# Split pieces stored by SP, early mixed tokens in a shared 8 KB buffer, and weights' high words in PSUM, in an attention and mixer kernel on one Trainium2 core

## The chip, the cores and the metric

The kernel runs on one core of one Trainium2 chip. The core has five engines that run side by side, each with its own list of instructions in fixed order: PE (matrix products, results into PSUM), DVE and ACT (elementwise work on SBUF and PSUM), POOL (elementwise work on SBUF) and SP (here it only issues DMA transfers). An engine waits at an instruction until the data or the buffer that it needs is there, and all that stands behind it on that engine waits too. The metric is the device time of one execution in microseconds (us); less is better.

## The reference, cut to what matters

Three blocks follow each other; all is fp32, B = 4, S = 576.

```python
# attention: 4 x 8 heads of 64, S = 576
scores = scale * q @ k.T + minimum(-(cum[:, None] - cum[None, :]), 0)   # causal
attn = softmax(scores)
x = (attn @ v)                                       # -> [4, 576, 512]
# mixer 1 (d_model 512, d_ff 1024)
xk = mu_k * x + (1 - mu_k) * x_prev                  # x_prev: x one token earlier
xr = mu_r * x + (1 - mu_r) * x_prev
k = maximum(xk @ w_k, 0)
x = sigmoid(xr @ w_r) * (k * k @ w_v)
# mixer 2
u = x + (maximum(x.T @ w_tok1, 0) @ w_tok2).T
out = u + maximum(u @ w_ch1, 0) @ w_ch2
```

## The kernel before, in words

Products of fp32 accuracy are made of three products of split numbers: a value is stored as a high part in the format fp32r and a low part (the rest), and `products` adds high x high, high x low and low x high. The weights come from the host as float64, read as pairs of 32-bit words. `weight_load` brings a piece (128 partitions x 512 values for w_k and w_r, x 256 for w_v) to SBUF, and `weight_split` makes high and low parts of it: ACT scales the high words (`high`) and the low words in place, DVE joins them with two shift-and-or instructions (lines 572 and 573), ACT copies the sum to the high part, and the rest is subtracted (line 577, POOL for w_k and w_r, DVE for w_v; w_v is halved first, by a copy of ACT).

Order of the work: the first batch's 8 heads are done twice over. `early` makes the first 256 queries of each head from plain fp32 products; `late` makes queries 256 to 575. Then 24 `visits` (the heads of batches 1 to 3, in pairs) do all 576 queries with split products (`scores`, `transposes`, `values`). Among them stand the products of mixer 1 (`up` gives the tile `h`, `gate` gives `r`, `down` gives `vd`), and later mixer 2. The order in each engine's list is set by a scheduler from places given by hand (`with at(...)`); it is fixed before the run.

The places that the change touches:

- `keep_busy` adds products whose result nobody reads (tile `idle`, in a PSUM bank of the pool `ps_d`), 4 after each of the 16 transposes of `early` and 3 after those of the first three heads of `late`.
- `mix` makes a tile of mixed tokens (`XK` for k, `XR` for r) with four operations: lines 478 and 479 on DVE, the high part on ACT (480), the low part on DVE (481). For the first chunk (256 tokens of batch 0) its four tiles are placed at N0 = 16, behind the early heads. `up` needs all four.
- `load` and `split` prepare the queries and keys of a pair of visits in four pieces of 128x288: SP loads a piece (`qkr`, two buffers), ACT copies the high part, POOL subtracts (line 224, `qkp`, two buffers) and POOL issues the store to DRAM (`hl_d`, line 225). `place` loads them back as the tiles `X` (lines 251 to 254, on SP), and `scores` uses these.
- The queries and keys of the first four early heads (`HL`) lie in 8 KB per partition of the pool `cp`.

Of the kernel before, what the change touches and what calls it, by code (L numbers as in the profile page):

```python
# [24 lines left out]
def attention_moe_mixer(  # L25
# [59 lines left out]
    ps_d = ctx.enter_context(tc.tile_pool(name="ps_d", bufs=2, space=PSUM, reuse_waits="tile"))  # L85

# [11 lines left out]
    act = {"ps": ps_d}  # L98
# [45 lines left out]
    xt = {}  # L144
# [7 lines left out]

    def keep_busy(n, x, w):
        for _ in range(n):
            nc.tensor.matmul(act["idle"][:, 0:w], x[:, 0:128], x[:, 0:w], start=True, stop=True)  # L155
# [8 lines left out]
    def bias_rows(cp):  # L164
# [3 lines left out]
        cum = cp.tile([G, S], F32, name="cum")  # L168
# [38 lines left out]

    def part(y):
        x, c = divmod(y, 2)
        return x, S * c // 2, S * (c + 1) // 2  # L210

    def load(i, y):
        g = visits[i][0]
        x, c0, c1 = part(y)
        t = qk_raw[i, y] = qk_p.tile([128, S // 2], F32, tag="raw", name="qkr", bufs=2)
        nc.sync.dma_start(out=t, in_=qk[g:g + 2, :, x, c0:c1].rearrange("h d s -> (h d) s"))

    def split(i, y):
# [3 lines left out]
        e = qk_p.tile([128, 2, S // 2], F32, tag="parts", name="qkp", bufs=2)  # L222
        copy("A", e[:, 1].bitcast(F32R), t)
        nc.gpsimd.tensor_tensor(out=e[:, 0], in0=t, in1=e[:, 1], op=ALU.subtract)
        nc.gpsimd.dma_start(out=hl_d[g:g + 2, :, 2 * x:2 * x + 2, c0:c1].rearrange("h d t s -> (h d) t s"), in_=e)
# [85 lines left out]
    def early(h, j, V0, cp):  # L311
# [14 lines left out]
        keep_busy(4, P, 128)  # L326
# [31 lines left out]
    def late(h, j):  # L358
# [19 lines left out]
        if h < 3 and m == 128:  # L378
            keep_busy(3, P, 128)
# [91 lines left out]

    def mix(b, c, i, p):
        dst = act[("XK", "XR")[i]]
# [3 lines left out]
        t = act["sm"].tile([128, CM], F32, tag="t", name="t", bufs=3)  # L477
# [5 lines left out]
    def up(b, c, m):  # L483
        n = width(c)
        kk, x = act["KK"], act["XK"]
# [81 lines left out]
    def weight_split(key, hi, lo, half=0):  # L567
        t = raw.pop(key)
        low, high = t[:, :, :, 0], t[:, :, :, 1]
        copy("A", f32(high), f32(high), 2.0 ** -112)  # L570
        nc.scalar.activation(out=low.bitcast(U32), in_=low.bitcast(U32), func=AF.Copy, scale=TOP3, bias=-0.496)  # L571
        nc.vector.scalar_tensor_tensor(out=low, in0=high, scalar=3, in1=low, op0=ALU.logical_shift_left, op1=ALU.bitwise_or)  # L572
        nc.vector.scalar_tensor_tensor(out=low, in0=high, scalar=-2 ** 31, in1=low, op0=ALU.bitwise_and, op1=ALU.bitwise_or)  # L573
        if half:
            copy("A", f32(low), f32(low), 0.5)
        copy("A", hi, f32(low))
        (nc.vector if half else nc.gpsimd).tensor_tensor(out=lo, in0=f32(low), in1=f32(hi), op=ALU.subtract)
# [91 lines left out]
    act["idle"] = ps_d.tile([128, 512], F32, tag="d", name="idle")  # L669
# [4 lines left out]
    early_at.append((cp.tile([128, 8 * QC], F32, name="HL"), 0, 4))  # L674
# [299 lines left out]
```

## Time and profile before

| | us |
|---|---|
| median of 3 runs | 893.46 (891.07 to 894.57) |
| the profiled execution, its own time | 887.59 |
| its span, first to last instruction | 885.8 |
| PE busy | 847.3 (96%) |
| DVE busy | 535.2 (60%) |
| ACT busy | 469.8 (53%) |
| POOL busy | 347.9 (39%) |

A busy time is the sum over an engine's instructions in the span. The shares are means over stages with different limits, so they are read by stretches of time below. The granted clock is the mean TensorE clock that the chip gave, as a share of 2.4 GHz.

### The profile page before, as it was taken

To read this page: it belongs to the slowest core of one execution; us is meant where nothing else is said; L and a number is where in the kernel's file an instruction comes from. 1 tells how busy PE (TensorE), PEld (TensorE's weight loads), DVE (VectorE), ACT (ScalarE), POOL (GpSimd) and SP (SyncE) were. 2 spreads that over 40 slices of the span, in tenths; PEclk is the share of its full clock that TensorE was granted. 3 is DMA by queue.
4 is the path that set the end of the run, shared out by engine and by line. 5 is a ranking of instruction groups with operands and counts; after the bars stand their busy time and mean duration, and the time that the engine had idled before them with its cause. 6 is when DMAs were issued, how large, how long until landed. Compare 5 with 4: busy or idle time off the path is not lost.

```text
span 885.8 us, 17817 instructions
## 1 busy us (share of the span) xinstructions
PE 847.3 (96%) x6185; PEld 793.4 (90%) x6185; DVE 535.2 (60%) x1583; ACT 469.8 (53%) x1320; POOL 347.9 (39%) x510
## 2 busy tenths in 40 slices
PE   7969999999789999999989899999999999999998
PEld 5736677998679999999989899899999999999998
DVE  4896897677899677996657866871331322222321
ACT  3877976866776765868456775760320211211210
POOL 3676876877773433645244674650000000000000
PEclk8969999999999999999999999999999999999999
DMA  7975667578753334441132656653022112112100
GB/s 195 255 207 170 205 188 215 163 215 245 199 159 85 82 79 107 100 121 48 50 100 80 206 157 197 208 186 124 25 71 63 44 40 66 38 42 67 43 25 24
DMA packets 78730, 108.37 MB, mean 122 GB/s; under 512 B 11072, under 2 KB 59200, under 8 KB 78640
## 3 DMA queue, kind: packets, MB, share of 16 engines
q1 hardware_dynamic: 68352, 77.40, 32.0%
q0 software_dynamic: 8416, 29.24, 10.2%
q8 instruction: 49, 0.80, 0.4%
q10 hardware_dynamic: 1872, 0.59, 0.4%
q14 instruction: 41, 0.34, 0.1%
HBM read 77.74 MB, written 28.90 MB: 120 GB/s over the span
## 4 chain that ended last, share of the span: by engine, by line
PE 70%; DVE 9%; DMA 7%; ACT 5%; issue 4%; POOL 3%; SPq 0%; ACTq 0%; POOLq 0%; DVEq 0%
PE c L110 32%; PE vd L110 8%; PE h L110 7%; PE r L110 4%; PE t L110 3%; PE t L411 3%; PE pv L463 3%; DMA hl_d<-qkp 2%; DMA raw<-in_moe_w_ch_dram 2%; DVE raw L572 2%; PE s L286 2%; PE pv L397 2%; PE s L287 2%; DVE raw L573 1%; PE s L368 1%
## 5 line engine op out<-in xcount | busy, mean ns | idle before, releaser
L813 ACT ACTIVATE HID<-c 128x256 fp32r<-128x256 f32 (+1 forms) x96 | 39.4, 410 | 218.7 <-PE c L110 218.5
L274 POOL TENSOR_SCALAR P<-P,sum 64x576 f32<-64x576 f32 (+4 forms) x160 | 101.2, 636 | 94.1 <-DVE sum L273 41.9
L110 PE MATMUL h<-XK,WK 128*128 128x256 f32 (+1 forms) x768 | 124.5, 302 | 4.1 <-ACT k L490 2.0
L110 PE MATMUL vd<-KK,WV 128*128 128x256 f32 (+1 forms) x768 | 121.6, 300 | 0.0
L110 PEld LDWEIGHTS h<-XK,WK 128*128 128x128 f32 x768 | 106.6, 188 | 10.1 <-ACT k L490 3.1
L271 ACT ACTIVATE P<-P,mx 64x576 f32<-64x576 f32 (+4 forms) x160 | 95.9, 600 | 28.5 <-DVE mx L261 27.5
L110 PEld LDWEIGHTS vd<-KK,WV 128*128 128x128 f32 x768 | 106.8, 188 | 1.7 <-issue 0.7
L110 PE MATMUL c<-U,WK 128*128 128x256 f32 (+1 forms) x768 | 102.6, 291 | 2.1 <-DVE HID L814 2.1
L110 PE MATMUL c<-HID,WV 128*128 128x256 f32 (+1 forms) x768 | 104.4, 291 | 0.0
L110 PEld LDWEIGHTS c<-U,WK 128*128 128x128 f32 x768 | 98.7, 188 | 2.4 <-DVE HID L814 2.3
L110 PEld LDWEIGHTS c<-HID,WV 128*128 128x128 f32 x768 | 100.4, 188 | 0.0
L814 DVE SCALAR_TENSOR_TENSOR HID<-c,HID 128x256 fp32r<-128x256 f32 (+1 forms) x96 | 43.9, 457 | 83.3 <-ACT HID L813 83.2
L878 DVE TENSOR_TENSOR ut<-c,ut 128x256 f32<-128x256 f32 (+1 forms) x32 | 14.7, 458 | 119.9 <-PE c L110 112.5
L261 DVE CUSTOM_DVE_ANT_0 P<-s,maskc 64x288 f32<-64x288 f32 (+4 forms) x160 | 74.9, 474 | 16.9 <-PE idle L155 4.4
L493 POOL TENSOR_TENSOR KK<-k,KK 128x256 fp32r<-128x256 f32 (+1 forms) x64 | 53.5, 837 | 34.7 <-ACT k L492 29.2
L110 PE MATMUL r<-XR,WR 128*128 128x320 f32 (+1 forms) x384 | 61.4, 302 | 2.6 <-ACT k L490 2.6
L75 ACT ACTIVATE raw<-raw 128x256 f32<-128x256 f32 (+2 forms) x101 | 46.8, 466 | 29.4 <-DMA raw<-in_moe_w_ch_dram 9.7
L572 DVE SCALAR_TENSOR_TENSOR raw<-raw 128x256 int32<-128x256 int32 (+2 forms) x85 | 49.7, 584 | 19.8 <-ACT raw L571 16.6
L110 PEld LDWEIGHTS r<-XR,WR 128*128 128x128 f32 x384 | 53.9, 192 | 3.6 <-ACT k L490 2.9
L411 PE MATMUL t<-ident,P 128*128 128x128 f32 (+1 forms) x360 | 52.8, 262 | 3.5 <-DVE PT L440 2.4
L110 PE MATMUL c<-HID,WR 128*128 128x256 f32 (+1 forms) x384 | 54.5, 291 | 0.0
L573 DVE SCALAR_TENSOR_TENSOR raw<-raw 128x256 int32<-128x256 int32 (+2 forms) x85 | 52.9, 624 | 1.2
(116 smaller groups left out, 1695.9 us busy)
## 6 DMA issues: line engine op xcount, KB each, us to landing
X<-hl_d SPq DMA_DIRECT2D x72, 288.0 KB
hl_d<-qkp POOLq DMA_DIRECT2D x48, 288.0 KB, 4.2
raw<-in_moe_w_ch_dram POOLq DMA_DIRECT2D x48, 256.0 KB, 3.7
qkr<-in_qk_dram SPq DMA_DIRECT2D x48, 144.0 KB
yt<-y_d SPq DMA_DIRECT2D x16, 288.0 KB
u_d<-yt SPq DMA_DIRECT2D x16, 288.0 KB
raw<-in_moe_w_k_dram SPq DMA_DIRECT2D x8, 512.0 KB
raw<-in_moe_w_v_dram SPq DMA_DIRECT2D x16, 256.0 KB
```

The costliest lines, as they stand in the source:

```text
L75: nc.scalar.activation(out=out, in_=in_, func=AF.Copy, scale=scale)
L110: nc.tensor.matmul(ps, a, b, start=first and i == 0, stop=last and i == n - 1)
L261: nc.vector.tensor_tensor_reduce(out=P[0:m, c0:c1], in0=ps[0:m, 0:c1 - c0], in1=maskc[0:m, 512 - q0 + c0:512 - q0 + c1], scale=-scale, sca ...
L271: nc.scalar.activation(out=P[0:m, 0:w], in_=P[0:m, 0:w], func=AF.Exp, bias=mx[0:m, x:x + 1], scale=-1.0, accum_out=sm[0:m, 0:1])
L274: nc.gpsimd.tensor_scalar(out=P[0:m, 0:w], in0=P[0:m, 0:w], scalar1=sm[0:m, 1:2], scalar2=1.0, op0=ALU.mult, op1=ALU.mult)
L411: nc.tensor.transpose(ps[0:r, p0 + m * k:p0 + m * k + m], P[0:m, 128 * k:128 * k + r], ident[0:m, 0:m])
L463: nc.tensor.matmul(ps[:, o:n], vv[:, k, :], part, start=(k == 0 and t == 0), stop=(k == nk - 1 and t == len(parts) - 1),)
L493: nc.gpsimd.tensor_tensor(out=kk[:, 1, m, 0:n], in0=t[:, 0:n], in1=f32(kk[:, 0, m, 0:n]), op=ALU.subtract)
L572: nc.vector.scalar_tensor_tensor(out=low, in0=high, scalar=3, in1=low, op0=ALU.logical_shift_left, op1=ALU.bitwise_or)
L573: nc.vector.scalar_tensor_tensor(out=low, in0=high, scalar=-2 ** 31, in1=low, op0=ALU.bitwise_and, op1=ALU.bitwise_or)
L813: nc.scalar.activation(out=hi, in_=ps, func=AF.Relu)
L814: nc.vector.scalar_tensor_tensor(out=lo, in0=ps, scalar=0.0, in1=f32(hi), op0=ALU.max, op1=ALU.subtract)
```

## The change

- The two banks of `ps_d` are no longer open from the start. In the first stage a pool `ps_w` has them, and for w_k and w_r ACT writes the scaled high words there (`high`) and not in place; the two DVE instructions read `high` from PSUM. `ps_d` opens after it. The `idle` tiles come from `ps_t`, the pool of the transposes; there are 3 and not 4 per early transpose, and only the first late head has any.
- One buffer of 8 KB (tag `HX`) is used in turn for the queries and keys of the first four early heads (`HE`), for the mixed k tokens of the first chunk (`HX`) and for all raw and split pieces of the visits (`PB`). Each user waits until the one before has been read.
- The first chunk's mixed tokens are placed among the early heads (3.5, 5.5, 7.5 and so on) and not behind them.
- Halving w_v goes into the copy to the high part (its scale) and into the subtraction, which becomes a multiply and subtract on DVE. One ACT copy per piece goes.
- The store of a split piece is issued by SP and not by POOL.

```diff
     def keep_busy(n, x, w):
+        idle = ps_t.tile([128, 512], F32, tag="t", name="idle")
         for _ in range(n):
-            nc.tensor.matmul(act["idle"][:, 0:w], x[:, 0:128], x[:, 0:w], start=True, stop=True)
+            nc.tensor.matmul(idle[:, 0:w], x[:, 0:128], x[:, 0:w], start=True, stop=True)
...
+    def stage():
+        if "PB" not in act:
+            act["PB"] = qk_p.tile([128, 8 * QC], F32, tag="HX", name="PB")
+        return act["PB"]
...
-        t = qk_raw[i, y] = qk_p.tile([128, S // 2], F32, tag="raw", name="qkr", bufs=2)
+        t = qk_raw[i, y] = stage()[:, y % 2 * S // 2:(y % 2 + 1) * S // 2]
         nc.sync.dma_start(out=t, in_=qk[g:g + 2, :, x, c0:c1].rearrange("h d s -> (h d) s"))
...
-        e = qk_p.tile([128, 2, S // 2], F32, tag="parts", name="qkp", bufs=2)
+        e = stage()[:, S + y % 2 * S:S + y % 2 * S + S].rearrange("p (t s) -> p t s", t=2)
         copy("A", e[:, 1].bitcast(F32R), t)
         nc.gpsimd.tensor_tensor(out=e[:, 0], in0=t, in1=e[:, 1], op=ALU.subtract)
-        nc.gpsimd.dma_start(out=hl_d[g:g + 2, :, 2 * x:2 * x + 2, c0:c1].rearrange("h d t s -> (h d) t s"), in_=e)
+        nc.sync.dma_start(out=hl_d[g:g + 2, :, 2 * x:2 * x + 2, c0:c1].rearrange("h d t s -> (h d) t s"), in_=e)
...
-        keep_busy(4, P, 128)
+        keep_busy(3, P, 128)
...
-        if h < 3 and m == 128:
+        if h < 1 and m == 128:
             keep_busy(3, P, 128)
...
+    def mixed(b, c, i):
+        if (b, c, i) == (0, 0, 0):
+            if "HX" not in act:
+                act["HX"] = qk_p.tile([128, 2 * KD * QC], F32R, tag="HX", name="HX")
+            return act["HX"].rearrange("p (t k s) -> p t k s", t=2, k=KD)
+        return act[("XK", "XR")[i]]
+
     def mix(b, c, i, p):
-        dst = act[("XK", "XR")[i]]
+        dst = mixed(b, c, i)
...
-    def weight_split(key, hi, lo, half=0):
+    def weight_split(key, hi, lo, half=0, ps=None):
         t = raw.pop(key)
         low, high = t[:, :, :, 0], t[:, :, :, 1]
-        copy("A", f32(high), f32(high), 2.0 ** -112)
+        if ps is None:
+            copy("A", f32(high), f32(high), 2.0 ** -112)
+        else:
+            bank = ps.tile([128, high.shape[1], high.shape[2]], I32, tag="w", name="high")
+            copy("A", f32(bank), f32(high), 2.0 ** -112)
+            high = bank
         nc.scalar.activation(out=low.bitcast(U32), in_=low.bitcast(U32), func=AF.Copy, scale=TOP3, bias=-0.496)
         nc.vector.scalar_tensor_tensor(out=low, in0=high, scalar=3, in1=low, op0=ALU.logical_shift_left, op1=ALU.bitwise_or)
         nc.vector.scalar_tensor_tensor(out=low, in0=high, scalar=-2 ** 31, in1=low, op0=ALU.bitwise_and, op1=ALU.bitwise_or)
+        copy("A", hi, f32(low), 0.5 if half else 1.0)
         if half:
-            copy("A", f32(low), f32(low), 0.5)
-        copy("A", hi, f32(low))
-        (nc.vector if half else nc.gpsimd).tensor_tensor(out=lo, in0=f32(low), in1=f32(hi), op=ALU.subtract)
+            nc.vector.scalar_tensor_tensor(out=lo, in0=f32(low), scalar=0.5, in1=f32(hi), op0=ALU.mult, op1=ALU.subtract)
+        else:
+            nc.gpsimd.tensor_tensor(out=lo, in0=f32(low), in1=f32(hi), op=ALU.subtract)
...
-    early_at.append((cp.tile([128, 8 * QC], F32, name="HL"), 0, 4))
+    early_at.append((qk_p.tile([128, 8 * QC], F32, tag="HX", name="HE"), 0, 4))
...
+        if h % 2 == 1 and h > 1:
+            with at(2 * h + 1.5):
+                for p in range(2) if h == 3 else (h // 2,):
+                    mix(0, 0, 0, p)
...
-            weight_split((nm, f), W[:, 0, :, f:f + 128], W[:, 1, :, f:f + 128])
+            weight_split((nm, f), W[:, 0, :, f:f + 128], W[:, 1, :, f:f + 128], ps=ps_w)
...
-    with at(N0):
-        for p in range(KD):
-            mix(0, 0, 0, p)
```

In the changed file the lines shift: 155 (fillers) is 157, 110 (products) is 108, 261 (row maximum) is 268, 368 and 377 (late scores and transposes) are 375 and 384, 478 to 481 (mix) are 492 to 495, 571 to 573 (shift and or) are 592 to 594, 577 is 597 and 599.

How the order changes, at three places. First PE, where the products `h` of the first chunk begin (`s<-X` and `t<-ident,P` are scores and transposes of `late`, `pv` its values). Before:

```order
L377 MATMUL t<-ident,P_923 128x128 x3
L155 MATMUL idle<-P_923 128x128 x3
L377 MATMUL t<-ident,P_965 128x128 x4
L155 MATMUL idle<-P_965 128x128 x3
L377 MATMUL t<-ident,P_984 128x64 x4
L377 MATMUL t<-ident,P_984 64x64
L368 MATMUL s<-X_510 64x288
L110 MATMUL h<-XK,WK 128x256 x4
L368 MATMUL s<-X_513 128x384
L110 MATMUL h<-XK,WK 128x256 x3
```

and after the change:

```order
L404 MATMUL pv<-PT_801,VV_536 64x64
L384 MATMUL t<-ident,P_925 128x128 x3
L108 MATMUL h<-HX,WK 128x256 x18
L384 MATMUL t<-ident,P_964 128x128
L108 MATMUL h<-HX,WK 128x256
```

`h` moves ahead of the second late head's last transposes and score, as one block of 18, and the fillers of that head are gone.

Second DVE, among the early heads, at a weight piece of w_k (`raw` is its buffer). Before:

```order
L77 COPY xt<-pv 128x256
L273 RECIPROCAL sum<-sum 128x1
L572 SCALAR_TENSOR_TENSOR raw<-raw 128x512
L261 ISA P_319,mx<-s,maskc 128x128
L261 ISA mx 128x1
L272 TENSOR_SCALAR sum<-sum 128x1
L573 SCALAR_TENSOR_TENSOR raw<-raw 128x512
```

and after the change:

```order
L492 TENSOR_SCALAR t<-xt,mu 128x256
L279 TENSOR_SCALAR sum<-sum 128x1
L493 SCALAR_TENSOR_TENSOR t<-xt,omu,t 128x256
L280 RECIPROCAL sum<-sum 128x1
L279 TENSOR_SCALAR sum<-sum 128x1
L268 ISA P_332,mx<-s,maskc 128x128
L268 ISA mx 128x1
L280 RECIPROCAL sum<-sum 128x1
L593 SCALAR_TENSOR_TENSOR raw<-high,raw 128x512
L268 ISA P_348,mx<-s,maskc 128x256
L268 ISA mx 128x1
L495 TENSOR_TENSOR HX<-t,HX 128x256
```

The operations of a mixed token tile stand here now, and the shift-and-or reads `high`. Third the pieces: before, POOL's list, among the last early heads and the first late one:

```order
L224 TENSOR_TENSOR qkp<-qkr,qkp 128x288 x2
L225 DMA hl_d<-qkp 128x2x288
L274 TENSOR_SCALAR P_448<-P_448,sum 128x256
L225 DMA hl_d<-qkp 128x2x288
L274 TENSOR_SCALAR P_791<-P_791,sum 128x384
```

and after the change SP's list, at the sixth late head, where the first pieces are loaded:

```order
L258 DMA X_1448<-ext_d 4x1152
L223 DMA PB<-in_qk_dram 128x288 x2
L575 DMA raw<-in_moe_w_v_dram 128x2x256 x2
L360 DMA VV_1244<-in_v_dram 128x4x128
L361 DMA VV_1244<-in_v_dram 64x128
L232 DMA hl_d<-PB 128x2x288
L223 DMA PB<-in_qk_dram 128x288
L232 DMA hl_d<-PB 128x2x288
L223 DMA PB<-in_qk_dram 128x288
```

The stores stand between the loads of SP, and the first piece comes at the sixth late head and not before the first.

## Rows read from the trace of the kernel before

**Rows 1.** The page, part 1: busy us, share of the span, instructions.

```profile
PE 847.3 (96%) x6185; PEld 793.4 (90%) x6185; DVE 535.2 (60%) x1583; ACT 469.8 (53%) x1320; POOL 347.9 (39%) x510
```

**Rows 2.** Busy us of PE, PEld, DVE, ACT, POOL by stretch; clock; DMA share, GB/s.

```profile
20.00:47.40 27.40, 27.25 (x177) 20.73 (x176) 22.64 (x73) 23.88 (x60) 18.99 (x24) 1.00 0.98 263
47.40:71.40 24.00, 15.75 (x74) 8.90 (x72) 20.58 (x42) 17.24 (x44) 18.12 (x18) 0.72 0.62 181
71.40:136.40 65.00, 63.33 (x391) 45.70 (x392) 55.06 (x152) 52.20 (x156) 45.52 (x62) 1.00 0.66 196
200.00:260.00 60.00, 52.97 (x372) 47.13 (x371) 50.72 (x197) 47.33 (x141) 46.37 (x68) 0.97 0.79 214
```

**Rows 3.** Waits of PE, 47.4 to 71.4 us: total us, times, longest.

```profile
PE s L368 <- DVE mx L261: 7.2, 3, 3.1
```

**Rows 4.** Timeline of DVE: start us, duration us, instruction.

```profile
40.48 0.68 DVE L261 CUSTOM_DVE_ANT_0 P<-s,maskc 128x512 f32<-128x512 f32 x1
...
47.21 2.60 DVE L572 SCALAR_TENSOR_TENSOR raw<-raw 128x512 int32<-128x512 int32 x1 [0.60 <-ACT raw L571]
...
56.65 0.68 DVE L572 SCALAR_TENSOR_TENSOR raw<-raw 128x512 int32<-128x512 int32 x1
...
64.07 0.96 DVE L573 SCALAR_TENSOR_TENSOR raw<-raw 128x512 int32<-128x512 int32 x1
```

**Rows 5.** Groups by form, 0 to 160 us: count, busy us, mean ns, idle before.

```profile
L75 ACT ACTIVATE raw<-raw 128x256 f32<-128x256 f32 x32 | 13.9, 439 | 11.0 <-DMA raw<-in_moe_w_v_dram 8.6 <-DVE raw L573 2.2
L577 DVE TENSOR_TENSOR WV<-raw,WV 128x256 fp32r<-128x256 f32 x16 | 12.8, 801 | 1.3 <-ACT WV L75 1.3
L572 DVE SCALAR_TENSOR_TENSOR raw<-raw 128x512 int32<-128x512 int32 x12 | 12.4, 1037 | 1.0 <-ACT raw L571 1.0
L573 DVE SCALAR_TENSOR_TENSOR raw<-raw 128x512 int32<-128x512 int32 x12 | 11.6, 971 | 0.1
...
L261 DVE CUSTOM_DVE_ANT_0 P<-s,maskc 128x512 f32<-128x512 f32 x10 | 6.8, 682 | 1.6 <-PE idle L155 0.8 <-PE t L377 0.7 <-PE s L287 0.2
```

**Rows 6.** Timeline of PE: start us, us from first to last, instructions.

```profile
23.25 1.05 PE L155 MATMUL idle<-P 128*128 128x128 f32 x8
24.14 0.38 PE L325 MATMUL t<-ident,P 128*128 128x128 f32 x2
...
71.40 1.11 PE L110 MATMUL h<-XK,WK 128*128 128x256 f32 x4 [0.41 <-ACT XK L480]
...
136.37 0.22 PE L286 MATMUL s<-X 128*128 128x128 f32 x1
```

**Rows 7.** The chain of waits in order of time: start us, us, what.

```profile
101.39 2.34 PE pv L397 x10
108.83 2.13 PE s L368 x6
111.45 1.38 PE r L110 x12
125.78 2.83 PE vd L110 x24
...
214.55 6.02 DMA X<-hl_d
225.89 4.77 DMA qkr<-in_qk_dram
```

**Rows 8.** Pieces (ns min/median/max, first and last start us), ACT's waits, landing.

```profile
L75 ACT ACTIVATE qkp<-qkr x36: 425/443/476, 102.3 to 251.2; 128x288 fp32r<-128x288 f32 x36
L224 POOL TENSOR_TENSOR qkp<-qkr,qkp x36: 785/805/1036, 103.1 to 252.0; 128x288 f32<-128x288 f32 x36
  DMA qkr<-in_qk_dram: 4.5, 4
...
L225 POOL DMA_DIRECT2D hl_d<-qkp x48: 725/756/918, 44.4 to 254.8; - x48
L253 SPq DMA_DIRECT2D X<-hl_d x24: 585/606/1581, 121.0 to 405.5; - x24
DMA to landing us min/median/max: 2.7/4.2/7.9
```

More of the change, by code (lines that the diff above doesn't have):

```diff
@@ L84, in attention_moe_mixer @@
     dram = ctx.enter_context(tc.tile_pool(name="dram", bufs=1, space=DRAM))
-    ps_d = ctx.enter_context(tc.tile_pool(name="ps_d", bufs=2, space=PSUM, reuse_waits="tile"))
     ident = const.tile([128, 128], F32, name="ident")
@@ L151, in constants, with behind @@
         make_identity(nc, ident)
+    def behind(p, cell):
+        nc.gpsimd.tensor_copy(cell, xt[0, p][0:1, 1:2])
     def keep_busy(n, x, w):
+        idle = ps_t.tile([128, 512], F32, tag="t", name="idle")
         for _ in range(n):
-            nc.tensor.matmul(act["idle"][:, 0:w], x[:, 0:128], x[:, 0:w], start=True, stop=True)
+            nc.tensor.matmul(idle[:, 0:w], x[:, 0:128], x[:, 0:w], start=True, stop=True)
     def mixes():
@@ L167, in bias_rows @@
         e32 = cp.tile([G, 2, 2, QC], F32, name="e32")
-        cum = cp.tile([G, S], F32, name="cum")
+        cum = st
         nc.gpsimd.memset(e32[:, 0, 0, :], 1.0)
@@ L476, in mix @@
         n = z - a
-        t = act["sm"].tile([128, CM], F32, tag="t", name="t", bufs=3)
+        t = act["mt"].tile([128, act["mtw"]], F32, tag="t", name="t", bufs=act["mtb"])
         nc.vector.tensor_scalar(out=t[:, 0:n], in0=x[:, 1 + a:1 + z], scalar1=mu[:, i, p:p + 1], scalar2=1.0, op0=ALU.mult, op1=ALU.mult)
@@ L484, in up @@
         n = width(c)
-        kk, x = act["KK"], act["XK"]
+        kk, x = act["KK"], mixed(b, c, 0)
         ps = act["ps"].tile([128, n], F32, tag="d", name="h")
@@ L553, in attention_moe_mixer, with weight_load @@
     raw = {}
-    def weight_load(key, sw, n, pool, tag, q=nc.sync):
+    def weight_load(key, sw, n, pool, tag, q=nc.sync, after=None):
         r, k, f = sw.shape
         t = pool.tile([128, n, 2], I32, tag=tag, name="raw")[:, 0:k * f].rearrange("p (k f) t -> p k f t", f=f)
+        if after is not None:
+            behind(after, f32(t[0:1, 0, 0:1, 0]))
         for r0 in range(0, 128, r):
@@ L668, in attention_moe_mixer @@
     nc.vector.memset(maskc, 0.0)
-    act["idle"] = ps_d.tile([128, 512], F32, tag="d", name="idle")
+    ps_s2, ps_w = open_pool(name="ps_w", bufs=2, space=PSUM, reuse_waits="tile")
     keep_busy(13, maskc, 512)
@@ L695, in after_bias @@
             early_bias(y, e32)
+    act["mt"], act["mtb"], act["mtw"] = cp, 1, QC
     constants()
+    with at(3):
+        mixes()
     for h in range(H):
@@ L703, in attention_moe_mixer @@
                 early(h, j, V0, cp)
+        if h % 2 == 1 and h > 1:
+            with at(2 * h + 1.5):
+                for p in range(2) if h == 3 else (h // 2,):
+                    mix(0, 0, 0, p)
     with at(2):
         split_bias(cp, cum)
-    with at(9):
-        mixes()
     with at(N0 - 5):
@@ L723, in attention_moe_mixer @@
     wst_s.close()
+    ps_s2.close()
+    ps_d = ctx.enter_context(tc.tile_pool(name="ps_d", bufs=2, space=PSUM, reuse_waits="tile"))
+    act["ps"] = ps_d
     ap_s, ap = open_pool(name="act", bufs=1, reuse_waits="tile")
```

3 lines of the change are left out of this document (2 added, 1 removed).

## The prediction, before the changed kernel had run

> **What bounds the kernel now.** I read the page's busy times first: PE is busy for 96% of the span [rows 1], so a change pays only where PE stands still, runs at the low clock, or does work that it need not do. The view by stretches of time says where that is [rows 2]. From 20 to 47.4 us PE has no gap and the clock is full. From 47.4 to 71.4 us it is busy for 15.75 of 24 us at a granted clock of 0.72, between its two levels (1.2 and 2.4 GHz): the engine had stood still for waits, and ran part of the stretch at the lower level. From 71.4 to 136.4 us it is busy for 63.33 of 65.0 us, from 200 to 260 us for 52.97 of 60 us. The waits of PE in the bad stretch have one name: 7.2 us on the row maximum of DVE (line 261) [rows 3]. DVE itself is busy for 20.58 of these 24 us [rows 2], and its timeline shows with what: one shift-and-or of a weight piece (lines 572 and 573, 128x512) takes 2.60 us at 47.21, while the row maximum of the same width takes 0.68 us [rows 4]. By form, the 24 such instructions take 24.0 us in all (12.4 + 11.6), 1.04 and 0.97 us on average [rows 5]. In the timeline the one at 56.65 takes 0.68 us [rows 4], so the excess over 0.67 us each is 24.0 - 16.1 = 7.9 us. The ones that are long read both tensors from SBUF; the row maximum, which reads one of its two from PSUM, takes 0.682 us on average over ten [rows 5]. So the front of the kernel waits for DVE, and DVE waits for something that only its instructions with two SBUF inputs meet.
>
> **Part 1: high words in PSUM.** All 24 instructions now read `high` from a PSUM bank. Bounds: nothing (they stay as slow), or 7.9 us of DVE time. I take 7.9, as the row nearest in kind (a PSUM and an SBUF input, 512 columns) is at 0.682 us with no spread to speak of. The twelve ACT copies that now write PSUM I cost at no change; the trace has no ACT write to PSUM, and a tenth of a microsecond either way on twelve is 1.2 us.
>
> The Trainium skill (SBUF — State Buffer, section "Who interferes with whom") states that a DVE instruction with two SBUF inputs contends with a GpSimd instruction that reads SBUF, and that one with at most one SBUF input does not; by it the whole 7.9 us goes, which is what the rows at 0.68 and 2.60 us suggest. The same skill (VectorE: DVE Perf Modes, section on the TRN2 errata) charges a PSUM source 120 cycles of fixed cost where an SBUF source has 58; that speaks against the change, an estimate of 24 x 62 cycles = 1.6 us more on DVE, and the sum would be 1.6 us less good. The trace does not show that surcharge: 0.68 us for both kinds at their shortest.
>
> **Part 2: fillers.** PE loses 16 idle products among the early heads (4 to 3 in each of 16 groups) and 12 among the late ones. Each is two passes; eight passes start at 23.25 and the next instruction at 24.14 [rows 6], 0.111 us a pass. That is 32 passes or 3.6 us before 47 us, and 24 passes or 2.7 us from 65 to 82 us. The fillers now take buffers of `ps_t`, whose earlier user must be read first; as the order puts the products that need the same copy right beside them, I cost that wait at nothing. If it isn't hidden, it is one copy of 128x384 a head.
>
> **Part 3: mixed tokens early, and when the first `h` can start.** `h` needs all four mixed token tiles and, as its PSUM banks were the weights' banks, the last two high words released. In the new order that is DVE's twelfth line-594 row, just behind the fourth `HX`. Before, the twelfth line-573 instruction ends at 64.07 + 0.96 = 65.03 us [rows 4]. The new order has six more mix operations of 256 columns ahead of it (half of 0.68 us each: 2.0 us) and 7.9 us less of stalls: 59.1 us, and I take 60. PE can be there: it was busy for 27.25 + 15.75 = 43.0 us from 20 to 71.4, of which 44 passes (4.9 us) go; 38.1 us fit into 40, less if the slow stretch runs at the full clock.
>
> From there to the first score of the visits PE needed 136.4 - 71.4 = 65.0 us [rows 6]. Of this go the 1.7 us of idle time [rows 2], 12 passes of filler (1.3 us) and 14 of the `vd` products, which now stand behind that score (24 take 2.83 us [rows 7], so 1.7 us); nine transposes and a 64x288 score, some 1.5 us, come in. That leaves 61.8 us: 121.8 instead of 136.4, a gain of 14.6, less the 1.7 us of `vd` that are only later, 12.9 us. ACT is the cover that may fail: it was busy for 52.2 of 65.0 us there [rows 2], and by the order it gets five instructions more (136 for 131) into 3 us less, with three times WR and three times WV among them; at 0.4 to 0.7 us each its share rises from 0.80 to 0.88. I keep back 3.4 us for waits of PE on ACT and DVE: 9.5 us.
>
> **Part 4: w_v.** Sixteen copies of 128x256 leave ACT, at 0.439 us [rows 5] 7.0 us over 100 us; the last DVE step keeps its two SBUF inputs and its 0.80 us [rows 5], now with a multiply in it. It is worth only what ACT's relief is, which is counted above: 14 of the sixteen stand in that stretch, 6.1 us, and with them ACT's share would be some 0.98.
>
> **Part 5: stores on SP.** POOL loses 48 issues of 0.756 us [rows 8], 36 us over the span, most of it slack: PE has no POOL wait among its long ones. SP waits for the subtraction before each store, and behind it stand the next load of a piece, X loads and w_v. The load of a piece had to wait for the same subtraction before, so nothing new is waited for; I cost it at nothing. What is later is the first piece: its buffer is the mixed tokens', so it is loaded after the last `h` of the first chunk, where before the first store left at 44.4 us [rows 8].
>
> **Rivals.**
> - *The late pieces stall PE (the rival on the other side).* Between the last `h` and the first visit's score PE has 48 `r` products (5.5 us at 1.38 for 12), 67 `vd` (7.9), three heads' scores (2.13 each) and values (2.34 each) [rows 7] and 36 transposes (some 4 us): 31 us. The chain of the four pieces is load 4.77, copy and subtraction 0.44 + 0.80, store 0.6 + 4.2 [rows 7, 8], a second round in the same buffers 0.44 + 0.80 + 0.80 + 0.6 + 4.2, then the X loads, 1.2 for two issues and 6.02: 25.6 us by medians, 33 with both stores at the longest, 7.9 us. With queueing on ACT and POOL a stall of 2 to 8 us is possible once; it leaves a gain of 2 to 7 us. It turns into a loss only if each pair of heads waits: one pair takes (405.5 - 121.0)/11 = 25.9 us [rows 8], and the rounds of four pieces some 17. Were they above 25.9, each microsecond costs eleven; at 27.5 us the time is 893.5 - 9.5 + 17.6 = 901.6. For it: the new order packs four pieces into about one visit. Against it: two rounds are well under a pair, and in the old trace ACT waited for the loads in 4 cases only.
> - *The PSUM source brings nothing,* or ACT is the real bound. Then `h` starts at 67, the fillers' 3.6 us and some idle time remain: gain 2.5 to 4, 889.5 to 891.
> - *More than that.* Nothing kept back (12.9), and part of the 7.0 us that PE stands still from 200 to 260 us goes too, as POOL has no stores there: a gain of 14 to 20, 873.5 to 879.5.
>
> **How the numbers follow.** The profiled execution took 887.59 us (span 885.8 and 1.8 around it); the median of the three runs is 893.46, 0.7% above it. The sum is made in the profile's time, 887.6 - 9.5 = 878.1, and I carry the difference over to the median: 884.0. Chances: the forecast (gain 5 to 14) 0.57, more 0.11, nothing from PSUM 0.15, late pieces 0.17 (0.07 of it near no change, 0.10 slower). 0.5% is 4.5 us, about what a measurement of this kernel can tell from no change. So faster 0.68, same 0.22, slower 0.10. The range reaches from 875 (most of the larger gain) to 892 (nothing from PSUM, and part of the stall); the likeliest case alone holds 879.5 to 888.5.
>
> **What would show it.** Part 1: all 24 instructions at 0.6 to 0.75 us. Part 3: the first `h` on HX near 60 us, the stretch before it without a low granted clock, and the first visit's score near 122 to 125. Part 2: 108 passes of fillers. Part 5: no DMA issue among POOL's rows, and the ends of PE's long waits not on X or hl_d. I am wrong if `high` comes late by ACT (PE waits for DVE as before, and DVE for line 592), if PE stands in front of the first visit's scores for more than 8 us, or if ACT waits for pieces again and again from 130 to 300 us.

## The result, and the profile after

The changed kernel takes 884.72 us (median of 17 executions, 880.22 to 893.88), the kernel before 892.46 us (17 executions, 888.26 to 896.27). The ratio is 0.9915, 95% interval 0.9889 to 0.9941: faster by 7.6 us, between 5.3 and 9.9. Forecast were 884.0 us and a gain of 9.5.

Nine executions of the changed kernel took 880.22 to 884.72 us at a mean granted clock of 0.980 to 0.986, and eight, the profiled one (889.3 us, clock 0.976) among them, took 886.74 us or more at 0.971 to 0.977. The profiled execution of before (887.59 us), in contrast, was quicker than all 17 that were measured of that kernel. So the two traces can't be set against each other by their ends; they have to be read stretch by stretch, and the same front has to be looked at in another execution.

First the page of the changed kernel, part 1, which answers to [rows 1]:

```profile
PE 850.6 (96%) x6129; PEld 791.3 (89%) x6129; DVE 517.6 (58%) x1583; ACT 466.4 (53%) x1304; POOL 312.0 (35%) x462
```

DVE is busy for 17.6 us less, POOL for 36. PE is not: its 56 passes of filler are gone, yet it was busy for 3.3 us more, because a busy PE at half clock counts in full. The same four stretches as in [rows 2]:

```profile
20.00:47.40 27.40, 23.33 (x111) 16.21 (x112) 17.82 (x67) 21.30 (x56) 12.03 (x16) 0.74 0.97 246
47.40:71.40 24.00, 21.46 (x79) 12.88 (x78) 17.05 (x50) 15.85 (x36) 10.14 (x11) 0.72 0.34 98
71.40:136.40 65.00, 64.81 (x402) 46.60 (x402) 53.27 (x158) 49.55 (x145) 35.90 (x47) 1.00 0.59 169
200.00:260.00 60.00, 48.84 (x343) 42.43 (x342) 48.81 (x188) 44.63 (x132) 37.12 (x55) 0.99 0.83 225
```

The first row is the surprise: the clock fell to 0.74 where it had been 1.00. In the last row PE is busy for 4.1 us less than before at about the same clock: this execution also stands still more among the visits. The DVE groups by form, 0 to 160 us, answer to [rows 5]:

```profile
L597 DVE SCALAR_TENSOR_TENSOR WV<-raw,WV 128x256 fp32r<-128x256 f32 x16 | 8.3, 521 | 0.0
...
L594 DVE SCALAR_TENSOR_TENSOR raw<-high,raw 128x512 int32<-128x512 int32 x12 | 8.2, 682 | 0.0
L593 DVE SCALAR_TENSOR_TENSOR raw<-high,raw 128x512 int32<-128x512 int32 x12 | 8.1, 676 | 3.2 <-ACT high L75 3.1
L268 DVE CUSTOM_DVE_ANT_0 P<-s,maskc 128x512 f32<-128x512 f32 x10 | 6.8, 684 | 2.1 <-PE t L384 1.9 <-PE s L294 0.2
```

The 24 instructions with a PSUM source take 8.2 + 8.1 = 16.3 us where they took 24.0, and now each takes about as long as the row maximum. Why the front was no earlier all the same, ACT's timeline shows (start, duration, instruction, idle time before it and what ended it):

```profile
28.94 0.66 ACT L592 ACTIVATE raw<-raw 128x512 uint32<-128x512 uint32 x1 [1.05 <-DMA raw<-in_moe_w_k_dram]
...
34.26 0.65 ACT L592 ACTIVATE raw<-raw 128x512 uint32<-128x512 uint32 x1 [2.34 <-DMA raw<-in_moe_w_k_dram]
34.81 0.47 ACT L75 ACTIVATE T<-t 128x384 f32<-128x384 f32 x1
```

ACT reaches the sixth piece of w_k before it has landed, stands for 2.34 us, and behind it in ACT's list stands the copy `T` of an early head. PE's timeline, with the first `h` and the first score of the visits ([rows 6] has them at 71.40 and 136.37):

```profile
35.34 1.54 PE L343 MATMUL pv<-T,V 128*64 128x256 f32 x4 [3.05 <-ACT T L75]
...
71.99 2.35 PE L108 MATMUL h<-HX,WK 128*128 128x256 f32 x18
...
132.72 0.33 PE L293 MATMUL s<-X 128*128 128x128 f32 x1 [0.19 <-DVE mx L268]
```

And by stretches of 5 us, columns as above:

```profile
30.00:35.00 5.00, 1.54 (x11) 1.08 (x9) 3.06 (x12) 2.66 (x9) 2.56 (x4) 0.83 0.92 162
35.00:40.00 5.00, 4.66 (x15) 3.22 (x16) 2.11 (x8) 3.76 (x11) 2.83 (x3) 0.50 0.70 207
40.00:45.00 5.00, 5.00 (x14) 2.38 (x13) 2.74 (x12) 4.26 (x11) 1.91 (x3) 0.50 1.09 276
45.00:50.00 5.00, 5.00 (x16) 3.21 (x16) 3.76 (x17) 4.52 (x10) 0.74 (x1) 0.50 0.99 272
50.00:55.00 5.00, 5.00 (x15) 2.91 (x14) 3.54 (x9) 0.99 (x3) 3.49 (x4) 0.50 0.79 250
55.00:60.00 5.00, 4.79 (x26) 3.84 (x27) 0.43 (x1) 3.33 (x7) 1.30 (x1) 0.78 0.12 43
```

PE stands still for most of 31 to 35 us, and then runs at 0.50, the lower level, for 20 us although it is busy throughout. The lead of this execution went with it: `h` starts at 72.0, and the first visit's score is still 3.7 us earlier than before.

### The profile page after: what moved, and what is told of

It reads as the page before. It is cut to its first block, busy times and chain, and to the rows that moved or that the text cites. A ratio compares the mean times of both kernels' runs of the same rounds, so it can differ in the third digit from the quotient of the medians.

```text
span 887.5 us, 17677 instructions
## 1 busy us (share of the span) xinstructions
PE 850.6 (96%) x6129; PEld 791.3 (89%) x6129; DVE 517.6 (58%) x1583; ACT 466.4 (53%) x1304; POOL 312.0 (35%) x462
## 3 DMA queue, kind: packets, MB, share of 16 engines
q1 hardware_dynamic: 81408, 91.56, 37.3%
q0 software_dynamic: 4576, 15.08, 5.4%
## 4 chain that ended last, share of the span: by engine, by line
PE 67%; DMA 12%; DVE 9%; ACT 5%; issue 3%; POOL 2%; SPq 1%; ACTq 0%; POOLq 0%; DVEq 0%
PE c L108 32%; PE h L108 8%; PE vd L108 7%; DMA PB<-in_qk_dram 6%; PE t L108 4%; PE r L108 4%; PE pv L470 2%; PE t L418 2%; PE s L375 2%; DMA raw<-in_moe_w_ch_dram 1%; DMA raw<-in_moe_w_k_dram 1%; DVE raw L593 1%; DVE raw L594 1%; PE s L293 1%; PE s L294 1%
## 5 line engine op out<-in xcount | busy, mean ns | idle before, releaser
L108 PE MATMUL h<-XK,WK 128*128 128x320 f32 (+1 forms) x672 | 108.5, 304 | 4.9 <-ACT XK L494 2.4
L108 PEld LDWEIGHTS h<-XK,WK 128*128 128x128 f32 x672 | 95.1, 191 | 7.5 <-ACT k L504 3.1
L231 POOL TENSOR_TENSOR PB<-PB 128x288 f32<-128x288 f32 x48 | 40.3, 841 | 37.8 <-ACT PB L75 36.7
L447 DVE TENSOR_TENSOR PT<-t,PT 128x384 fp32r<-128x384 f32 (+1 forms) x96 | 44.8, 468 | 14.5 <-ACT PT L446 12.4
L108 PE MATMUL c<-U,C1A 128*128 128x256 f32 (+1 forms) x384 | 52.8, 296 | 0.0
```

The costliest lines, as they stand in the source:

```text
L108: nc.tensor.matmul(ps, a, b, start=first and i == 0, stop=last and i == n - 1)
L447: nc.vector.tensor_tensor(out=low, in0=pv, in1=f32(view(PT[0])), op=ALU.subtract)
```

## The experiments

The theory at the outset: the gain is made in the front, most of it by the PSUM source. The rival: DVE has slack there, and the loads of the weights, which ACT waits for, set the pace; then the other parts carry the gain. The times below are medians; ratios are to the kernel before on the same chip (median 890.54 us beside runs 1, 2, 5 and the fillers of 3; 890.76 beside the rest of 3, 4 and 6; 892.12 beside 7 and 8), with their 95% intervals. A difference of two ratios is uncertain by about 0.0035 to 0.0045, that is 3 to 4 us. One thing holds for every run: the scheduler orders all lists anew, so behind an edit the other rows can stand in another order too (six buffers change no row of PE, and yet PE's list differs from 38 us on; with the stores on POOL it differs from 111 us on). A difference in time is that of the edit together with its new order.

**1. High words in SBUF again.**

```diff
-            weight_split((nm, f), W[:, 0, :, f:f + 128], W[:, 1, :, f:f + 128], ps=ps_w)
+            weight_split((nm, f), W[:, 0, :, f:f + 128], W[:, 1, :, f:f + 128])
```

> The changed kernel with one part undone: ACT scales the high words in place in SBUF again, and both shift-and-or instructions read two SBUF tensors; all else is as changed. Theory (the PSUM source is the largest part of the gain): the 24 instructions take 1.0 us on average again and not 0.68, about 7.5 us more on DVE before 70 us; the first h starts later than in the changed kernel, PE waits longer for the row maximum, and the time goes back to 889 to 894 us. Rival (the loads of the weight pieces and ACT pace the front, DVE has slack in it): the instructions are longer, but the time stays at the changed kernel's 880 to 889 us.

Measured: 887.16 us, 0.9959 (0.9936 to 0.9982). DVE's groups by form in that kernel:

```profile
L594 DVE SCALAR_TENSOR_TENSOR raw<-raw 128x512 int32<-128x512 int32 x12 | 12.3, 1022 | 0.0
L593 DVE SCALAR_TENSOR_TENSOR raw<-raw 128x512 int32<-128x512 int32 x12 | 10.2, 853 | 0.0
```

```profile
PE s L375 <- DVE mx L268: 4.7, 3, 2.4
```

6.2 us more on DVE, PE waits for the row maximum from 20 to 71.4 us for 4.7 us where the changed kernel's trace has 2.3, and the end is later by 0.0044, 3.9 us (0.8 to 7.0). The time lies below the theory's 889 to 894 us. And one expectation failed outright, that the first `h` would start later:

```profile
25.74 0.36 PE L108 MATMUL h<-HX,WK 128*128 128x256 f32 x1
```

Without weights in the two banks the scheduler put 18 of the 96 products `h` of the first chunk among the early heads, before 53 us. So not all else was as changed: the 3.9 us are the price of the source and of this other order together, and this run can't say which share of the gain hangs on the source.

**2. Only the high words in PSUM.** The kernel before with these lines of the change (the branch on `ps` in `weight_split` as there) and nothing else:

```diff
     def keep_busy(n, x, w):
+        idle = ps_t.tile([128, 512], F32, tag="t", name="idle")
...
+    ps_s2, ps_w = open_pool(name="ps_w", bufs=2, space=PSUM, reuse_waits="tile")
...
-            weight_split((nm, f), W[:, 0, :, f:f + 128], W[:, 1, :, f:f + 128])
+            weight_split((nm, f), W[:, 0, :, f:f + 128], W[:, 1, :, f:f + 128], ps=ps_w)
```

> The kernel before with one part of the change: the high words of w_k and w_r go to the two PSUM banks, and the fillers' tile moves to the pool of the transposes for it, but with their old number (4 and 3); mixed tokens, pieces, stores and w_v stay as before. Theory (PSUM source): the 24 instructions take 0.67 to 0.69 us, the PE waits for the row maximum between 47 and 71 us fall from 7.2 us to 3 or less, and the time is 4 to 7 us under the kernel before. Rival (the gain comes from the mixed tokens' place and the fewer fillers): the instructions are as short, but h can't start earlier, since its mixed tokens stand behind the early heads; less than 3 us.

Measured: 887.25 us, 0.9971 (0.9948 to 0.9994): 2.6 us, between 0.5 and 4.6. The 24 instructions take 0.684 us on average, and from 47.4 to 71.4 us PE waits for the row maximum for 3.7 us where it had waited 7.2 [rows 3]:

```profile
PE s L368 <- DVE mx L261: 3.7, 2, 2.7
```

`h` starts at 65.63 us. What the theory says of the front came out nearly, and against the rival `h` does start earlier; but the gain is of the rival's size. This is the cleanest measure of the source, about a third of the gain.

**3. The other parts undone one by one.** First the fillers in their old number:

```diff
-        keep_busy(3, P, 128)
+        keep_busy(4, P, 128)
...
-        if h < 1 and m == 128:
+        if h < 3 and m == 128:
```

> The changed kernel with the fillers in the old number: 4 and not 3 after each early transpose, 3 after those of three late heads and not of one. Theory (the fillers that went were PE time on the path, 6.3 us at full clock by the sum): 3 to 6 us slower than the changed kernel, 886 to 890 us in the median. Rival (they fill waits that PE has anyway and keep the clock up): the same or faster, with fewer executions of a mean clock under 0.978.

Then the mixed tokens at N0 again:

```diff
-        if h % 2 == 1 and h > 1:
-            with at(2 * h + 1.5):
-                for p in range(2) if h == 3 else (h // 2,):
-                    mix(0, 0, 0, p)
...
+    with at(N0):
+        for p in range(KD):
+            mix(0, 0, 0, p)
```

> The changed kernel with the mixed tokens of the first chunk placed behind the early heads again (N0), still in the shared buffer; all else as changed. Theory (their early place lets h start as soon as the last weight piece is split): the first h starts 3 to 6 us later than in the changed kernel, PE waits for it or runs late scores in its place, and the time is 3 to 5 us over the changed kernel's, 886 to 888 us. Rival (h waits for the last weight pieces anyway, which the DMA engines set, so the mix operations fit in behind): within 1.5 us of the changed kernel.

Then the copy that halves w_v:

```diff
-        copy("A", hi, f32(low), 0.5 if half else 1.0)
+        if half:
+            copy("A", f32(low), f32(low), 0.5)
+        copy("A", hi, f32(low))
...
```

The lines left out make the subtraction a plain one on DVE again.

> The changed kernel with w_v halved by an ACT copy of its own again (16 copies of 0.44 us, 7.0 us on ACT between 38 and 170 us) and subtracted without the multiply. Theory (ACT's relief counts where ACT was busy for 0.76 of the stretch from 71 to 136 us): 1 to 3 us slower than the changed kernel. Rival (ACT has slack there, PE was busy for 64.8 of 65 us): within 1 us of the changed kernel.

Measured: 885.77 us, 0.9944 (0.9922 to 0.9967); 885.27 us, 0.9937 (0.9915 to 0.9959); 885.29 us, 0.9943 (0.9924 to 0.9963). Against the changed kernel's 0.9915 these are 2.6, 2.0 and 2.5 us slower, each less than its own uncertainty of some 3 us. All four undone parts (run 1 and these three) point the same way, but only run 1 is clear of the noise. With mixed tokens placed late `h` still starts at 65.19 us, so the expected 3 to 6 us didn't come, as that run's rival has it for the front; its time (2.0 us slower, for less than 1.5) decides nothing.

**4. Stores on POOL again.**

```diff
-        nc.sync.dma_start(out=hl_d[g:g + 2, :, 2 * x:2 * x + 2, c0:c1].rearrange("h d t s -> (h d) t s"), in_=e)
+        nc.gpsimd.dma_start(out=hl_d[g:g + 2, :, 2 * x:2 * x + 2, c0:c1].rearrange("h d t s -> (h d) t s"), in_=e)
```

> The changed kernel with the 48 stores of split pieces issued by POOL again (0.756 us each, 36 us of POOL's time from 105 to 285 us). Theory (POOL has slack, the stores' place is worth nothing): within 1.5 us of the changed kernel, no wait of PE on POOL longer than 1.5 us. Rival (POOL's issues stand in front of subtractions and of the products with 1/sum that PE's transposes need): 2 to 5 us slower, with more PE waits on POOL from 130 to 280 us.

Measured: 879.77 us, 0.9869 (0.9836 to 0.9902), faster than the changed kernel by 4.1 us (uncertain by 3.7), which neither side had expected. ACT's waits from 95 to 290 us, first of the changed kernel, then of this one (what waited, for what: total us, times, longest):

```profile
ACT PB L75 <- DMA PB<-in_qk_dram: 28.9, 22, 3.1
```

```profile
ACT PB L75 <- DMA PB<-in_qk_dram: 6.4, 5, 2.0
```

This kernel does a second service. Up to `h` its lists are those of the changed kernel, row for row, so its trace is another execution of the same front:

```profile
31.95 0.66 ACT L592 ACTIVATE raw<-raw 128x512 uint32<-128x512 uint32 x1
32.51 0.47 ACT L75 ACTIVATE T<-t 128x384 f32<-128x384 f32 x1
```

```profile
49.79 1.54 PE L343 MATMUL pv<-T,V 128*64 128x256 f32 x4 [2.92 <-ACT T L75]
...
66.60 1.65 PE L108 MATMUL h<-HX,WK 128*128 128x256 f32 x12
...
127.02 0.22 PE L293 MATMUL s<-X 128*128 128x128 f32 x1
```

```profile
20.00:47.40 27.40, 25.14 (x155) 18.43 (x154) 23.64 (x86) 22.83 (x60) 14.58 (x19) 1.00 0.98 249
47.40:71.40 24.00, 21.31 (x83) 12.95 (x84) 16.58 (x47) 19.13 (x48) 11.73 (x12) 0.64 0.34 101
```

Here the sixth piece was there when ACT came at 31.95 us, 2.3 us earlier than in the changed kernel's own trace. The full clock lasts to 47 us, `h` starts at 66.6 and the first visit at 127.0, 9.4 us ahead of [rows 6]. But a stop of PE for the same copy follows at 46.9 to 49.8 us, and the clock falls there. What the theory says of PE came out (its longest wait for POOL is 0.9 us). One thing stays untested: the pages count 9216 more DMA packets in the two dynamic queues with the stores on SP (81408 + 4576) than with them on POOL (68352 + 8416), and no run tells what these cost.

**5. Six buffers for the pieces of w_k and w_r.**

```diff
-    wst_s, sp = open_pool(name="wst", bufs=5)
+    wst_s, sp = open_pool(name="wst", bufs=6)
```

> The changed kernel with six buffers in place of five for the pieces of w_k and w_r, so that the sixth piece is loaded with the first ones and not when the first buffer comes free. In the profile of the changed kernel ACT stands still for 2.34 us until that piece lands at 34.2 us, PE waits 3.05 us for the copy behind it, and the granted clock is 0.50 from 35 to 55 us. Theory (this late piece costs the executions with a mean clock of 0.971 to 0.977 their 6 to 8 us): no such wait, full clock from 30 to 55 us, the first h before 66 us, and all executions at 878 to 884 us with a mean clock of 0.98 or more. Rival (another wait takes its place, as the DMA engines are busy through this stretch): the times spread over 880 to 892 us as those of the changed kernel.

Measured: 882.42 us, 0.9914 (0.9881 to 0.9947), executions from 878.16 to 888.03: no change. The stop at 32 us is gone in its trace, as it was with five buffers in run 4's, the clock is full from 20 to 47 us, and the later stop is there:

```profile
51.63 1.54 PE L343 MATMUL pv<-T,V 128*64 128x256 f32 x4 [3.40 <-ACT T L75]
```

The rival of this run holds in the main: the times still spread, over 10 us, and there is another wait.

**6. Six buffers, and the first two pieces of w_v later.**

```diff
-                weight_load((k, f), rows(w_v, k, k + 2)[:, :, f:f + 128], S // 2, xt_p, "xt")
+                weight_load((k, f), rows(w_v, k, k + 2)[:, :, f:f + 128], S // 2, xt_p, "xt", after=3 if x < 21 else None)
```

> The changed kernel with six buffers for the pieces of w_k and w_r (as before) and, beyond that, the first two pieces of w_v loaded only after the last early head (POOL writes one element of the buffer from the last xt tile, so the load waits for it). Theory (the DMA engines, busy for 0.95 to 1.0 of the stretch from 20 to 50 us, pace the front, and half a megabyte of w_v stands in front of w_r's pieces there): ACT waits less for w_k and w_r, PE's stop of 3.4 us near 50 us in the run with six buffers shrinks below 2 us, the first h starts before 64 us, and the time is 2 to 4 us below the run with six buffers, 878 to 880 us beside a kernel before of 890.5. Rival (the front is set by DVE, or PE's stop by the order of ACT's work and not by the loads): as with six buffers alone, 881 to 884 us.

Measured: 885.74 us, 0.9939 (0.9910 to 0.9968). PE's timeline and its waits from 20 to 71.4 us in the profiled execution (881.11 us):

```profile
59.89 1.33 PE L108 MATMUL h<-HX,WK 128*128 128x256 f32 x9
...
124.76 0.22 PE L293 MATMUL s<-X 128*128 128x128 f32 x1
```

```profile
PE s L375 <- DVE mx L268: 1.2, 1, 1.2
PE pv L343 <- ACT T L75: 1.0, 1, 1.0
```

The front came out as the theory has it (the clock from 47.4 to 71.4 us is 0.93). In both kernels with this edit, here and in run 8, PE's stop for the copy `T` is 0.8 to 1.0 us, and with six buffers alone it is 2.9 to 3.4: half a megabyte less in front of w_r's pieces, with the order that comes with it, takes the stop away. The time did not follow: `h` stands 6.7 us and the first visit 2.3 us ahead of run 4's trace, and nothing measurable of it is left at the end.

**7. Why do the stores on SP cost, if they do?** The pieces' copies three steps further back:

```diff
-                if j < 4 and i + 2 < len(visits):
-                    split(i + 2, j)
-                    if j < 2:
-                        load(i + 2, 2 + j)
+                if j < 2 and i + 2 < len(visits):
+                    load(i + 2, 2 + j)
+            with at(N0 + n + 3.1):
+                if j < 4 and i + 2 < len(visits):
+                    split(i + 2, j)
```

> The changed kernel, stores on SP, with the place of the pieces' copies and subtractions (split) three steps later (3.1 for 0.1 behind the step's place), so that they stand further back in ACT's list; their loads keep their place. In the changed kernel ACT stands still for 28.9 us in 22 places at these copies until a piece has landed, in the one with stores on POOL for 6.4 us in 5. Theory A (the stores on SP moved the copies forward in ACT's list, ACT reaches them before the piece is there, and the exponentials and copies that PE needs are late): ACT's waits for pieces fall below 15 us and the time below the changed kernel's by 2 to 5 us, 878 to 881 beside a before of 890.5. Theory B (the stores on SP's own queue hold up the other loads, or their packets load the DMA engines): no gain, 882 to 885 us, also where ACT waits less.

In this code the third and fourth piece of a pair are written over the first and second before these are split, so the first two split pieces hold the later ones' values, and their copies also wait for the later loads; the instructions are the same in number. And the copies on POOL:

```diff
-        copy("A", e[:, 1].bitcast(F32R), t)
+        copy("P", e[:, 1].bitcast(F32R), t)
```

> The changed kernel, stores on SP, with the pieces' copies to the high part on POOL and not on ACT (48 of them, some 0.8 us each on POOL as the subtraction of the same size takes 0.80 us, and 21 us less on ACT). Theory A: ACT no longer stands at pieces at all, POOL does, which has the slack that the stores left; 2 to 6 us faster than the changed kernel. Theory B: the loads and stores are as late as before; within 1.5 us of the changed kernel, or slower where POOL's products with 1/sum now stand behind pieces (PE waits on POOL over 5 us in all).

Measured: 889.24 us, 0.9989 (0.9961 to 1.0017), and 887.15 us, 0.9960 (0.9936 to 0.9985), both slower than the changed kernel. In the first, ACT's waits at the pieces only change their name: 15.7 us for loads and 13.4 us for stores, where the changed kernel has 28.9, so it doesn't test theory A. In the second they are gone, and POOL waits 33.9 us for the loads in their place; from 95 to 300 us PE's transposes wait 3.6 us for POOL where they had waited 1.1. So the standing at the pieces brings nothing when it is moved from ACT to POOL. What it would bring to have it on no engine is not shown, and theory B isn't shown either.

**8. Stores on POOL with the better fronts.** The edits of runs 4 and 5, and of runs 4 and 6, together:

> The changed kernel with two edits: the stores of split pieces on POOL again, and six buffers in place of five for the pieces of w_k and w_r. If the stores' return is worth what one run of it showed (ratio 0.987 for 0.9915 of the changed kernel) and it has nothing to do with the front, it is worth the same here: 877 to 880 us beside a before of 890.5, a ratio of 0.985 to 0.989. If that run was chance, the ratio is that of six buffers alone, 0.991.

> As the one with stores on POOL and six buffers, and the first two pieces of w_v loaded only after the last early head. With stores on SP this last edit brought the first h to 59.9 us and the first score of the visits to 124.8 us, but the time was 885.7 us (ratio 0.994). If the lead was lost to the stalls that go with the stores on SP: 874 to 878 us, ratio 0.982 to 0.986. If a lead in the front is given back among the visits anyway (DVE and ACT busy for 0.8 of the stretch from 200 to 260 us): no better than with six buffers alone.

Measured: 889.57 us, 1.0002 (0.9972 to 1.0032), and 888.49 us, 0.9972 (0.9944 to 1.0001). With six buffers, the stores on POOL make the kernel slower by 0.0088, 7.8 us (uncertain by 4), where with five they had made it faster by 4.1; with six and w_v later the difference, 2.9 us slower, is within its uncertainty of 3.6. So the gain of run 4 is not the store's engine as such. The stretch from 220 to 240 us, first with five buffers, then with six (both with stores on POOL):

```profile
220.00:240.00 20.00, 17.43 (x108) 14.58 (x107) 18.80 (x69) 16.16 (x48) 16.94 (x25) 0.91 0.95 242
```

```profile
220.00:240.00 20.00, 14.43 (x77) 12.03 (x78) 16.00 (x64) 14.81 (x45) 14.18 (x21) 0.79 0.72 188
```

3.0 us more of standing still and a lower clock in the same 20 us: 77 products for 108. From the profiled executions, in us; PE idle and the granted clock are those from the first visit to the last:

| kernel | first `h` | first visit | last visit | first to last | PE idle | clock | its time |
|---|---|---|---|---|---|---|---|
| before | 71.4 | 136.4 | 420.0 | 283.7 | 11.1 | 0.99 | 887.6 |
| changed | 72.0 | 132.7 | 421.8 | 289.1 | 14.4 | 0.99 | 889.3 |
| high words in SBUF (1) | 25.7 | 130.6 | 416.1 | 285.5 | 10.2 | 0.99 | 883.0 |
| only PSUM (2) | 65.6 | 131.7 | 417.9 | 286.2 | 10.8 | 0.97 | 883.4 |
| fillers (3) | 66.5 | 135.2 | 419.6 | 284.4 | 10.4 | 0.96 | 885.4 |
| mixed tokens late (3) | 65.2 | 128.8 | 419.6 | 290.8 | 11.4 | 0.97 | 888.6 |
| w_v copy (3) | 64.6 | 126.0 | 417.0 | 291.0 | 11.4 | 0.96 | 885.2 |
| stores on POOL (4) | 66.6 | 127.0 | 412.3 | 285.3 | 9.0 | 0.98 | 881.7 |
| six buffers (5) | 65.0 | 126.5 | 416.7 | 290.3 | 13.1 | 0.98 | 885.3 |
| six, w_v later (6) | 59.9 | 124.8 | 410.9 | 286.1 | 12.7 | 0.99 | 881.1 |
| pieces' copies later (7) | 66.7 | 127.4 | 423.7 | 296.3 | 15.2 | 0.97 | 891.5 |
| copies on POOL (7) | 66.4 | 127.6 | 417.8 | 290.2 | 13.8 | 0.98 | 887.4 |
| POOL, six (8) | 61.6 | 128.4 | 422.8 | 294.4 | 14.9 | 0.96 | 889.4 |
| POOL, six, w_v later (8) | 60.0 | 124.5 | 414.6 | 290.1 | 13.6 | 0.98 | 882.8 |

(A visit is named by its first score.) Nine of the thirteen altered kernels bring the first visit to 124.5 to 128.8 us, some 8 to 12 us ahead of before. From there to the last visit they take 285 to 296 us, where before it was 283.7 (by the prediction's sum 1.7 us of that are `vd` products that now stand behind the first score). In the changed kernel's trace PE stands still for longer at the same clock, in the w_v copy's it has the lower clock alone, in the slowest two both.

## Why the prediction was right

The time (884.0 for 884.72) and the sign are right, and the gain of 9.5 us lies within the measured 5.3 to 9.9. The steps were not all right, and that the number came out so near is in part luck: a loss in the front that was not foreseen met a reserve that was kept for something else.

- *Part 1* was right to 0.2 us: 7.7 us of DVE time for 7.9 forecast. The twelve writes to PSUM by ACT cost nothing: 0.633 us for 0.672 in place. What the long instructions had met can be read from POOL's rows at the same times: before, all 13 of the 24 that took 0.70 us or more ran while POOL was at work, and the 7 that met no instruction of POOL took 0.67 to 0.69; in the changed kernel 15 meet POOL, and none takes over 0.692. Of the two statements of the Trainium skill that were weighed, the trace agrees with the one of SBUF — State Buffer ("Who interferes with whom"): in the changed kernel the 24 instructions lie between 0.662 and 0.692 us, while the shift-and-or with two SBUF inputs that is left (w_v's, 128x256) still averages 0.515 and 0.682 us, above the 0.41 us of the shorter ones in the timeline. The dearer PSUM source that the Trainium skill states (VectorE: DVE Perf Modes, TRN2 errata) doesn't show: 0.676 and 0.682 us, against 0.66 for the shortest of before with two SBUF inputs and 0.68 for the one in [rows 4].
- *Part 3* failed in its first step, "PE can be there: ... 38.1 us fit into 40, less if the slow stretch runs at the full clock". The sum took DVE as the only thing that the front waits for. With DVE relieved, ACT comes to the weight pieces before they have landed (the DMA engines' share from 20 to 47.4 us is 0.97 and 0.98 in two traces, and was 0.98 before), a copy for PE stands behind, and the low clock stays: 0.64 to 0.72 from 47.4 to 71.4 us. In run 4's trace DVE ends its last shift-and-or for `h` at 63.6 us, and PE gets to `h` 3 us later. `h` starts at 66.4 to 66.7 us in three traces of this front, and at 72.0 in a fourth, where the stop came some 15 us sooner. Forecast was 60. Run 6 shows the forecast's `h` (59.9) and first score (124.8 for 122 to 125), once the pieces land earlier.
- The *reserve* of 3.4 us is the term that saved the sum, in another place than it was meant for. The first score at 127.0 instead of 121.8 is 5.2 us. With the 1.7 us of `vd` that is only later, 136.4 - 127.0 - 1.7 = 7.7 us of lead are left, and 7.6 were measured. That they agree shows little: the 127.0 is from run 4's trace, whose kernel measured faster than the changed one by 4.1 us, and in the changed kernel's own trace the score comes at 132.7, and the lead is gone by the last visit.
- *That the lead stays a lead* was taken for granted, and is not so. From first to last visit the sum implies 283.7 + 1.7 = 285.4 us. Of the nine altered kernels with an early first visit only two (285.3 and 286.1) stay within a microsecond of that. The kernel with six buffers and the stores on POOL has the 24 short instructions, the early mixed tokens, fewer fillers and its `h` at 61.6 us, and its ratio is 1.0002: so the parts that the sum prices don't fix the time, and something that no run isolates, of which the order of the lists is one candidate, weighs as much as the whole gain.
- *Part 2*: the passes are 6.3 us of PE time; given back, they cost 2.6 us, uncertain by 3. That part of them stands where PE would wait anyway would explain it, but isn't shown. *Part 4*, a relief of ACT: the copy costs 2.5 us when given back, also uncertain by 3, so it can't be told from nothing. Its last DVE step, priced at 0.80 us, takes 0.521; the multiply isn't the reason, as the plain subtraction takes 0.542 in the w_v copy kernel.
- *Part 5*, at nothing, is not confirmed. One pair of kernels says that the stores on SP cost 4.1 us, another that they bring 7.8, a third nothing clear; between the pairs the front's buffers, its loads and the order of the lists differ. What the move does to PE is left open.
- *The rivals.* The late pieces never stalled PE itself (in the changed kernel it waits 0.8 us for an X and 0.2 us for a piece's store), so the rival on the other side didn't come. But its sign did, "ACT waits for pieces again and again": 22 times, 28.9 us. As a sign of loss it was badly chosen, since the second kernel of run 7 took these waits off ACT, onto POOL, without a gain. (The chain priced there adds up to 24.9 us by its rows, not 25.6; nothing rests on it.) "The PSUM source brings nothing" falls by run 2. The other half of that rival, that ACT is the real bound and `h` starts at 67, fits the front (66.4 to 66.7, with ACT standing at pieces of weights), but not the gain: it gave 2.5 to 4 us.

What stays open is why the 23 visits take up to 12 us more in one altered kernel than in another. The table says how much of it is standing still and where the clock is low; which wait starts it, and how much is the order of the lists alone, no run separated.

## What to carry to other kernels

Where several engines are near 0.8 busy, taking the longest wait away can bring up the next one, here on transfers that had been just in time: before counting a stall as gained, look at what each in-order engine meets next, and whether that has landed. A lead at the start of a long stretch is worth only what the stretch doesn't give back; read it again at the stretch's end. Take more than one trace of the changed kernel's front before believing either: here the profiled execution hid the gain. And where a scheduler orders the lists anew for each edit, taking one part out is not a clean test: look where the rows of the other parts have gone.

## What the runs showed of the hardware

After a stop of 3.05 us TensorE was granted 0.50 of its clock for 20 us in which it was busy for 4.66 to 5.00 of each 5 us. In that execution, where one landing came 2.3 us late, `h` started 5.3 to 5.6 us later than in the three others of the same front. Other standing still did not do that: in run 6 PE was busy for only 51.89 of the 60 us from 200 to 260, at a granted clock of 1.00, where run 3's w_v kernel had 53.31 us at 0.86:

```profile
200.00:260.00 60.00, 51.89 (x372) 44.62 (x371) 51.22 (x194) 48.01 (x146) 39.44 (x56) 1.00 0.84 231
```

```profile
200.00:260.00 60.00, 53.31 (x340) 47.87 (x339) 47.95 (x179) 41.98 (x126) 34.49 (x50) 0.86 0.79 212
```

And 24 DVE instructions that had spread from 0.66 to 2.60 us shrank to a band of 0.03 us when one of two inputs moved to PSUM, and spread to 3.24 us again in run 1, where both were back in SBUF.
